# Threshold attention feeding an attention mixture of experts on one core: a new work order, a third pair of score banks at first, additions as reductions, masks in a row

## The chip, the cores and the metric

The kernel runs on one core of one Trainium2 chip. The metric is the device time of one execution in microseconds. A core has a matrix engine (TensorE, PE in the profile; its weight loads are PEld), a vector engine (VectorE, DVE), an activation engine (ScalarE, ACT), a general engine (GpSimd, POOL) and a queue engine (SyncE, SP) that issues DMAs. Matrix products are written to PSUM, which has eight banks of 128 partitions x 512 f32 values.

## The reference

Eight batches, eight heads, 576 rows, 64 values a head. The first stage is attention in which a score counts only when it lies within `tau` of its row's maximum. Its output, 576 x 512 a batch, is the input of the second stage: four experts, each a causal attention with its own projections, of which every row uses two.

```python
def _attn_ref(q, k, v, tau):
    scores = scale * np.matmul(q, k.transpose(0, 1, 3, 2))
    thresh = np.max(scores, axis=-1, keepdims=True) - tau
    scores = np.where(scores >= thresh, scores, -1000000000.0)
    ...
    attn = np.exp(scores)
    attn = attn / (np.sum(attn, axis=-1, keepdims=True) + 1e-09)
    return np.matmul(attn, v)

def _moe_ref(x, w_gate, wq, wk, wv, wo):
    logits = x @ w_gate
    topk = np.argpartition(-logits, K, axis=-1)[..., :K]
    ...
    for e in range(E):
        q = x @ wq[e]
        ...
        scores = scale * (q @ k.transpose(0, 2, 1))
        scores = np.where(causal, -1000000000.0, scores)
        ...
        ye = a @ v @ wo[e]
        ...
            out += mask[..., None] * w[:, :, kk:kk + 1] * ye
```

## The kernel before

**Tiling.** Two heads make a head pair; there are 32 (`n` = 0 to 31, four a batch). The 576 rows are four tiles of 128 and a tail of 64; the tails of both heads share one tile (tile 4). The order of the tiles is `TS` = 4, 2, 3, 0, 1, and `TS0` for the first pair.

**First stage**, for each pair: `load` (DMAs of q, k, v), `prep` (transposes of k and q, split into a high and a low f32r part by `hi` on ScalarE and `lo` on VectorE, and spread by DMAs to `kt` and `qt`), then `scores` for each tile. `scores` has, for each head: matmuls into a score buffer of two banks (`s_main`, or `s_tail` for the tail); the row maximum (`s_max`, L889, VectorE; scores carry a minus sign, so it is a minimum); exp on ScalarE (`s_exp`, L901); the threshold (`s_thr`, L894: an addition of `tau_p`, one for both heads); the masked multiply, which also adds up the rows (`s_stt`, L906, VectorE); the sum plus 1e-9 (`add_eps`, L911), its reciprocal (`inv`, L915); the division on GpSimd (`s_nrm`, L919); transposes on TensorE (L774) and their evacuation to `pt` and `ptt` (L763 on ScalarE, L765 on VectorE). `attnv` multiplies groups of tiles, (4, 2, 3) and (0, 1), with v. These matmuls have 64 output columns and stand side by side in the array: form 128\*64 in the profile, `cols="C"` in the code. All others are of form 128\*128, `"F"`, except the very first scores, `"R"`.

**Second stage**, `second(b)`, once a batch: projections (`proj`, `values`), the gate, scores of two experts at a time (`s2`: for each expert two f32r matmuls and, accumulated onto them, one bf16 matmul that adds the causal mask), maximum (`max2`, L1107), exp with row sums (`exp2`, L1115), `add_eps` and `inv` again, the scaling on GpSimd (`scale2`, L1135), transposes, `av2` (form 128\*64), and the output projection.

**Order.** The order of all instructions is written out by a planner. `work` makes a list of tasks, each with an engine, a time, dependencies, buffers and a due time `pri`, counted in fifths of a head pair: five units a pair, 20 a batch. `plan` runs them through a clock of its own: an engine that becomes free takes the ready task with the smallest `pri` for which buffers are free. On TensorE a task of another form than the last has `STICK` added to its `pri`, and when it is taken, `SWITCH` (ns) is added to its start. `PR` holds one offset for each kind of task, `PR0` corrections for the first four pairs; `PJ`, `VJ`, `S2J` and `TAILK` space the tasks of the second stage. The emitted order is fixed; on the chip, semaphores alone decide when an instruction starts.

**PSUM.** `Space.pick` gives banks: a score buffer (class `s`) takes a pair of neighbouring banks out of the first `SCAP` = 4, any other buffer (class `g`) one of the banks from `GFROM` = 4. `LEAVE` banks must stay free when scores take theirs. `EARLY` = 0.0, so the two other limits in these lines are not used.

**Other buffers.** `SLOTS` has the counts: 10 `pt`, 5 `ptt`, 4 `pp`, 8 `sm`. An `sm` is a 128 x 8 tile of row statistics: maxima in columns 0 and 1, sums in 2 and 3, thresholds in 4 and 5. The weights of the second stage are loaded in four parts, from `W_FROM` on, `W_EACH` apart, in the planner's ns.

Of the kernel before, what the change touches and what calls it, by code (L numbers as in the profile page):

```python
# [20 lines left out]
EPS = 1e-9  # L21

B, H, S, D = 8, 8, 576, 64
E = 4
# [56 lines left out]
CROSS, LATE, SELF, DRAIN, SWITCH, BEGIN = 40.0, 171.0, 36.0, 168.0, 120.0, 800.0  # L81


class Space:
# [177 lines left out]
def work(K):  # L262

    tasks = []

    def task(eng, t, fn, deps=(), pri=0.0, takes=(), uses=(), cols=None, ld=0.0, name="", at=0.0):
        t = t if isinstance(t, dict) else {eng: t}
        x = Task({e: (u[0] - u[1], u[0]) for e, u in t.items()}, fn, deps, pri, takes, uses, cols, ld, name, at)
        tasks.append(x)
        return x  # L270
# [34 lines left out]
    def load(n):  # L305
# [5 lines left out]
        dk = [dma(lambda j=j: K.load_k(n, j), (), pri, [ki], name=f"ldk{n}") for j in range(2)]  # L311
        dk.append(dma(lambda: K.load_kt(n), (), pri, [kit], move=144.0, name=f"ldk{n}"))
        dq = [dma(lambda j=j: K.load_q(n, j, e), (), pri + 0.01, [qi], name=f"ldq{n}", e=e) for j in range(2)]
        dq.append(dma(lambda: K.load_qt(n, e), (), pri + 0.01, [qit], move=144.0, name=f"ldq{n}", e=e))
        at = 20000.0 * n
        dv = [dma(lambda: K.load_v(n, vm), (), pri + 2, [vm], move=736.0, at=at, name=f"ldv{n}")]
        for j in range(2):
            dv.append(dma(lambda j=j: K.load_vt(n, vm, j), (), pri + 2, [vm], move=72.0, at=at, name=f"ldv{n}"))
# [3 lines left out]
        sc = task("DVE" if n == 0 else "POOL", (270, 30), lambda: K.scale_qt("DVE" if n == 0 else "POOL"), dq[2:], 5 * (n - 1) - 1, [], [qit], name=f"qs{n}")  # L322
# [10 lines left out]
    def prep(n):  # L333
# [4 lines left out]
        m = pe(4 * TR, lambda: K.tr_main(g, "k"), dk[:2], p0, [g, hl], [ki], ld=30.0, name=f"qkT{n}")  # L338
        hk, lk = split(g, slice(KO + ST, KO + ST + SM), [m], p0, hl, SM, f"hl{n}")
        g2 = Buf("g")  # L340
        m2 = pe(2 * TR, lambda: K.tr_tail(g2), [dk[2], sc], p0 + 0.5, [g2], [kit, qit], ld=30.0, name=f"qkTt{n}")
# [888 lines left out]
```

## Time and profile before

| what | value |
|---|---|
| median of three runs | 964.48 us |
| lowest, highest | 963.38, 966.53 us |
| profiled execution | 962.86 us |
| its span | 961.1 us |
| PE busy in it | 925.4 us, 9372 matmuls |
| DVE busy | 786.1 us, 2211 instructions |
| ACT busy | 629.6 us |
| POOL busy | 365.8 us |

The span runs from the first to the last instruction of the profiled execution. Busy times are sums over the whole span; a matmul's end is modelled, and the matmuls overlap, so a busy PE need not be at its peak. In rows of the timeline the columns are start, length, engine, line, operation, output<-input, shapes and count; neighbouring instructions of one kind are merged into one row, and what stands in brackets is the idle time before it and what ended it. In rows of the groups they are line, engine, operation, names and shapes, count, then busy time in us and mean length in ns, then the idle time before them and what ended it. A row of the waits has the waiting engine, tile and line, what it waited for, and total us, times and longest us. L774 and L777 are the helpers that issue every transpose and every other matmul, L763 and L765 every copy.

### The profile page before, as it was taken

Reading aid. Unit: us, or ns where it says so; the run is one execution under the profiler, and the core shown is the slowest. Engines: PE = TensorE matmul, PEld = TensorE weight load, DVE = VectorE, ACT = ScalarE, POOL = GpSimd, SP = SyncE. Lnnn points to the kernel's source line nnn. Section 1 sums busy time; section 2 is a strip of 40 time slices with the busy share of each in tenths; the row PEclk is TensorE's granted clock in tenths of the full one; section 3 lists DMA queues with packets and bytes.
Section 4 is the critical chain, followed back from the end, with each engine's and each line's share of the span. In section 5 each row is a group of like instructions: output and inputs, shape, how many; then the busy total and the mean of one; then the engine's idle time right before and its main releaser. Section 6 shows DMA issues by size and latency. Waiting matters only on the chain.

```text
span 961.1 us, 26069 instructions
## 1 busy us (share of the span) xinstructions
PE 925.4 (96%) x9372; PEld 847.2 (88%) x9372; DVE 786.1 (82%) x2211; ACT 629.6 (66%) x1468; POOL 365.8 (38%) x637
## 2 busy tenths in 40 slices
PE   5878999999999999999999999999999999999997
PEld 4767899989998899988999899998999889998985
DVE  4889888898888888888798987989888888888453
ACT  3677657676676666666676766766667676676454
POOL 2456334334243433434244433434324343343222
PEclk9999999999999999999999999999999999999999
DMA  6667663545646464554537466354564545531241
GB/s 143 150 174 167 155 152 88 133 102 156 148 118 145 106 151 117 136 144 113 138 90 170 109 153 150 87 128 118 152 153 109 134 105 149 129 95 45 60 113 61
DMA packets 148335, 121.26 MB, mean 126 GB/s; under 512 B 98288, under 2 KB 106480, under 8 KB 148208
## 3 DMA queue, kind: packets, MB, share of 16 engines
q1 hardware_dynamic: 146864, 119.31, 50.9%
q8 instruction: 75, 1.23, 0.6%
q10 hardware_dynamic: 1344, 0.30, 0.2%
q14 instruction: 52, 0.43, 0.1%
HBM read 30.42 MB, written 9.44 MB: 41 GB/s over the span
## 4 chain that ended last, share of the span: by engine, by line
PE 75%; DVE 17%; ACT 2%; issue 2%; DMA 1%; POOL 1%; SPq 0%; ACTq 0%; DVEq 0%; POOLq 0%
PE g L777 42%; PE g L774 19%; PE s L777 14%; DVE sm L889 5%; DVE pp L906 4%; DVE sm L1107 2%; DVE pt L765 1%; DVE sm L911 1%; ACT pt L763 1%; POOL pp L919 1%; DVE ptt L765 0%; DVE gs L1063 0%; DMA qit<-in_q_dram 0%; DMA ob<-in_moe_wv_dram 0%; DVE x L771 0%
## 5 line engine op out<-in xcount | busy, mean ns | idle before, releaser
L919 POOL TENSOR_SCALAR pp<-pp,sm 128x576 f32<-128x576 f32 x288 | 212.7, 749 | 320.4 <-DVE sm L915 238.1
L889 DVE TENSOR_REDUCE sm<-s 128x1 f32<-128x576 f32 x304 | 228.0, 753 | 31.7 <-PE s L777 20.2
L906 DVE SCALAR_TENSOR_TENSOR pp<-s,sm,pp 128x576 f32<-128x576 f32 x288 | 228.2, 815 | 18.2 <-ACT pp L901 8.6
L901 ACT ACTIVATE pp<-s,sm 128x576 f32<-128x576 f32 x288 | 213.8, 743 | 38.1 <-DVE sm L889 32.4
L763 ACT ACTIVATE pt<-g 128x512 f32<-128x512 f32 (+2 forms) x315 | 176.7, 583 | 77.3 <-PE g L774 74.2
L774 PE MATMUL g<-ident,pp 128*128 128x128 f32 x1312 | 192.7, 276 | 11.8 <-POOL pp L919 4.3
L777 PE MATMUL s<-kt,qt 128*128 128x288 f32 x1016 | 195.7, 315 | 6.9 <-DVE pp L906 6.6
L774 PEld LDWEIGHTS g<-ident,pp 128*128 128x128 f32 x1312 | 153.2, 141 | 22.1 <-POOL pp L919 7.8
L777 PEld LDWEIGHTS s<-kt,qt 128*128 128x128 f32 x1016 | 147.1, 191 | 15.3 <-issue 4.3
L777 PE MATMUL g<-pt,vm 128*64 128x128 f32 (+1 forms) x2560 | 156.0, 264 | 0.0
L777 PEld LDWEIGHTS g<-pt,vm 128*64 128x64 f32 x2560 | 132.9, 137 | 6.0 <-issue 4.5
L1135 POOL TENSOR_SCALAR p<-p,sm,gw 128x256 f32<-128x256 f32 (+4 forms) x144 | 89.8, 633 | 109.0 <-DVE sm L894 44.8
L777 PE MATMUL g<-x,wh 128*128 128x288 f32 x512 | 107.1, 302 | 0.0
L1115 ACT ACTIVATE p<-g,sm 128x512 f32<-128x512 f32 (+3 forms) x128 | 66.7, 527 | 33.2 <-DVE sm L1107 13.2
L777 PEld LDWEIGHTS g<-x,wh 128*128 128x128 f32 x512 | 81.5, 189 | 0.1
L777 PE MATMUL g<-x,wl 128*128 128x288 f32 x256 | 75.5, 295 | 0.0
L763 ACT ACTIVATE x<-g 128x320 fp32r<-128x320 f32 x64 | 26.2, 410 | 71.3 <-PE g L777 71.2
L771 DVE TENSOR_TENSOR x<-g,x 128x320 fp32r<-128x320 f32 x64 | 29.2, 456 | 48.4 <-ACT x L763 48.4
L765 DVE COPY pt<-g 128x512 f32<-128x512 f32 (+1 forms) x85 | 55.8, 658 | 15.3 <-PE g L774 14.0
L777 PE MATMUL g<-wh,x 128*128 128x260 f32 x320 | 65.0, 290 | 0.1
L777 PE MATMUL g<-qq 128*128 128x512 f32 (+3 forms) x256 | 61.8, 352 | 1.5 <-ACT p L1115 0.5
L774 PE MATMUL g<-ident,p 128*128 128x128 f32 x400 | 62.0, 279 | 0.9 <-POOL p L1135 0.9
(125 smaller groups left out, 1474.1 us busy)
## 6 DMA issues: line engine op xcount, KB each, us to landing
kt<-hl SPq DMA_DIRECT2D x248, 144.0 KB, 2.6
qq<-k SPq DMA_DIRECT2D x64, 256.0 KB, 4.4
qt<-hl SPq DMA_DIRECT2D x124, 128.0 KB, 2.5
ki<-in_k_dram SPq DMA_DIRECT2D x64, 128.0 KB, 3.3
vm<-in_v_dram SPq DMA_DIRECT2D x32, 256.0 KB, 3.1
qq<-q SPq DMA_DIRECT2D x64, 128.0 KB, 2.3
out_dram<-ob SPq DMA_DIRECT2D x32, 256.0 KB, 2.2
qi<-in_q_dram SPq DMA_DIRECT2D x62, 128.0 KB, 2.7
```

The costliest lines, as they stand in the source:

```text
L763: self.nc.scalar.activation(dst, src, AF.Copy)
L765: self.nc.vector.tensor_copy(dst, src)
L771: eng.tensor_tensor(dst, a, b.bitcast(F32), op=ALU.subtract)
L774: self.nc.tensor.transpose(out, x, self.ident)
L777: self.nc.tensor.matmul(out, x, y, start=first, stop=last)
L889: self.nc.vector.tensor_reduce(self.small(sm)[:, j:j + 1], self.dbank(s)[:, :, :HS], axis=AX.XY, op=op, negate=neg)
L901: self.nc.scalar.activation(e, self.dbank(s)[:, :, :HS], AF.Exp, bias=self.small(sm)[:, j:j + 1], scale=-1.0)
L906: self.nc.vector.scalar_tensor_tensor(e, self.dbank(s)[:, :, :HS], m[:, 4 + j:5 + j], e, op0=ALU.is_le, op1=ALU.mult, accum_out=m[:, 2 + j ...
L919: self.nc.gpsimd.tensor_scalar(p, p, self.small(sm)[:, 2 + j:3 + j], 0.0, op0=ALU.mult, op1=ALU.add)
L1107: self.nc.vector.tensor_reduce(o, v, axis=AX.X, op=ALU.max, negate=True)
L1115: self.nc.scalar.activation(self.p2(p2)[:, j * SM:j * SM + w], self.bank(gs[j])[:, o:o + w], AF.Exp, bias=m[:, j:j + 1], accum_out=m[:, 2 ...
L1135: self.nc.gpsimd.tensor_scalar(p, p, self.small(sm)[:, 2 + j:3 + j], g[:, o:o + 1], op0=ALU.mult, op1=ALU.mult)
```

## The change

Six things are changed.

1. **Prices and penalties of the planner**: `SWITCH`, `STICK`, `TAILK`, `PJ`, `S2J`, `TS0`, `W_FROM`, `W_EACH`, `LEAVE`.
2. **Due times**: `TUNE` holds some 400 corrections, one for a kind of task and a phase (the pair's place in the batch, in the first batch apart; first, middle or last batch), or a kind and a part (tile, expert pair). `tuned` looks them up by the task's name, which therefore gets separators, and `task` adds them to `pri`.
3. **Banks**: up to 56.7 us of the planner's clock, scores have three pairs (banks 0 to 5) and other buffers the banks 6 and 7; afterwards two pairs and four banks, as before. Banks 4 and 5 come from a pool of their own, which is closed and opened anew with single banks at the first use by a `g` buffer.
4. **Additions**: an `sm` is now a standing tile of 128 x 16, in which `tau` and 1e-9 are written once, next to each maximum and each sum. `s_thr` and `add_eps` become a `tensor_reduce` with `add` over two neighbouring values (`pairs`).
5. **Set-up**: GpSimd writes 1e-9 into the eight `sm` tiles (a memset each) and `tau` (two one-column operations each); the two VectorE operations for `tau_p` go.
6. **Masks**: `s2` issues the score matmuls of both experts first and then both mask matmuls. Where both experts share a bank (`nar`), the start flag is on the first expert's first matmul alone.

```diff
-CROSS, LATE, SELF, DRAIN, SWITCH, BEGIN = 40.0, 171.0, 36.0, 168.0, 120.0, 800.0
+CROSS, LATE, SELF, DRAIN, SWITCH, BEGIN = 40.0, 171.0, 36.0, 168.0, 172.0, 800.0
...
-            pairs = [i for i in range(0, SCAP if now > EARLY else 6, 2) if ok[i] and ok[i + 1]]
+            pairs = [i for i in range(0, 4 if now > EARLY else 6, 2) if ok[i] and ok[i + 1]]
...
-        one = [i for i in range(GFROM if now > EARLY else 2, 8) if ok[i]]
+        one = [i for i in range(4 if now > EARLY else 6, 8) if ok[i]]
...
+    def tuned(name):
+
+        if "/" in name:
+            f, b, *part = name.split("/")
+            phase = "a" if b == "0" else "z" if int(b) == B - 1 else "m"
+        elif "." in name:
+            f, n, *part = name.split(".")
+            phase = ("a" if int(n) < NPAIR else "") + str(int(n) % NPAIR)
+        else:
+            return 0.0
+        return TUNE.get(f"{f}|{phase}", 0.0) + (TUNE.get(f"{f}.{part[0]}", 0.0) if part else 0.0)
...
+        pri += tuned(name)
...
-                a = pe(2 * (f32r(2, w) + 68), lambda: K.s2(gs, nar, qq, t, w), sp, pri, list(dict.fromkeys(gs)), [qq], name=f"s2{b}")
+                a = pe(f32r(4, w) + 165, lambda: K.s2(gs, nar, qq, t, w), sp, pri, list(dict.fromkeys(gs)), [qq], name=f"s2/{b}/{ep}{t}")
...
-PJ = 0.62
+PJ = 0.619
 VJ = 0.56
-S2J = 1.29
-TAILK = 0.36
-STICK = 0.59
+S2J = 1.289
+TAILK = 0.733
+STICK = 0.794
...
+TUNE = {'sk2|a': -2.42, 'sk2|m': -1.16, 'sk2|z': 11.93, 'qs|a3': 10.37, 'max.4': 2.28, 'exp|2': 3.69,
...
-W_FROM = 31527.09
-W_EACH = 10736.66
+W_FROM = 35537.903
+W_EACH = 14490.379
 T2S = (3, 4, 2, 1, 0)
-TS0 = (2, 4, 3, 0, 1)
-LEAVE = 1
-SCAP = 4
-GFROM = 4
-EARLY = 0.0
+TS0 = (2, 4, 3, 1, 0)
+LEAVE = 0
+EARLY = 56700.0
...
+        self.third = tc.tile_pool(name="ps3", bufs=1, space=PSUM)
+        self.pool3, self.begun = self.third.__enter__(), EARLY > 0.0
...
-        self.tau_p = const([P, 2], F32, "tau_p")
-        for j in range(2):
-            nc.vector.tensor_scalar(self.tau_p[:, j:j + 1], tau_t, 0.0, None, op0=ALU.max)
...
+        self.sms = [const([P, 16], F32, f"sm{i}") for i in range(SLOTS["sm"])]
+        for t in self.sms:
+            nc.gpsimd.memset(t[:, 5:8:2], EPS)
...
+        for t in self.sms:
+            for j in range(2):
+                nc.gpsimd.tensor_scalar(t[:, 2 * j + 1:2 * j + 2], tau_t, 0.0, 0.0, op0=ALU.max, op1=ALU.add)
...
+            if buf.cls in "sg" and buf.slot in (4, 5):
+                if buf.cls == "g" and self.begun:
+                    self.third.__exit__(None, None, None)
+                    self.third, self.begun = self.tc.tile_pool(name="ps4", bufs=1, space=PSUM), False
+                    self.pool3 = self.third.__enter__()
+                pool = self.pool3
...
+    def pairs(self, sm, out, o, nj):
+
+        m = self.small(sm)
+        self.nc.vector.tensor_reduce(m[:, out:out + nj], m[:, o:o + 2 * nj].rearrange("p (j k) -> p j k", k=2), axis=AX.X, op=ALU.add)
...
-        self.nc.vector.tensor_tensor(m[:, 4 + a:4 + b], m[:, a:b], self.tau_p[:, a:b], op=ALU.add)
+        self.pairs(sm, 8 + js[0], 2 * js[0], len(js))
...
-    def add_eps(self, sm, o, nj):
-        x = self.small(sm)[:, o:o + nj]
-        self.nc.vector.tensor_tensor(x, x, self.eps[:, :nj], op=ALU.add)
...
+    def add_eps(self, sm, nj):
+        self.pairs(sm, 10, 4, nj)
...
-                self.mm(g[:, o:o + w], u[:, j, t * P:w], u[:, 2 + 2 * j + x, :w], x == 0, False)
-            self.mm(g[:, o + t * P:o + w], self.ident_b, self.mask, False, True)
+                self.mm(g[:, o:o + w], u[:, j, t * P:w], u[:, 2 + 2 * j + x, :w], x == 0 and not (nar and j), False)
+        for j in range(2):
+            o = j * w if nar else 0
+            self.mm(self.bank(gs[j])[:, o + t * P:o + w], self.ident_b, self.mask, False, j == 1 or not nar)
```

More of the change, by code (lines that the diff above doesn't have):

```diff
@@ L321, in load @@
         VMB[n] = vm
-        sc = task("DVE" if n == 0 else "POOL", (270, 30), lambda: K.scale_qt("DVE" if n == 0 else "POOL"), dq[2:], 5 * (n - 1) - 1, [], [qit], name=f"qs{n}")
+        sc = task("DVE" if n == 0 else "POOL", (270, 30), lambda: K.scale_qt("DVE" if n == 0 else "POOL"), dq[2:], 5 * (n - 1) - 1, [], [qit], name=f"qs.{n}")
         LD[n] = (ki, qi, kit, qit, vm, dk, sc, dv, dq)
@@ L355, in prep @@
                 sk[j] = [dma(lambda j=j, r=r: K.spread_k(hl, kt, j, r, None), tl if j == 0 else tl[:4],
-                             p0 + 1.6 + 0.1 * j, [kt], [hl], name=f"sk{n}", move=1288.0) for r in range(2)]
+                             p0 + 1.6 + 0.1 * j, [kt], [hl], name=f"sk.{n}", move=1288.0) for r in range(2)]
             else:
@@ L393, in scores @@
         th = [task("DVE", SMALL, lambda js=js: K.s_thr(sm, js), [ms[j] for j in js], i + PR["thr"], [], [sm],
-                   name=f"thr{n}_{s}") for js in ([[0, 1]] if nj == 2 and ONETHR else [[j] for j in range(nj)])]
+                   name=f"thr.{n}.{s}") for js in ([[0, 1]] if nj == 2 and ONETHR else [[j] for j in range(nj)])]
         for j in range(nj):
             ns.append(task("DVE", (825, 75), lambda j=j: K.s_stt(bufs[j], sm, pp, j), [es[j], th[j if len(th) > 1 else 0]], i + PR["stt"], [],
-                           [bufs[j], sm, pp], name=f"stt{n}_{s}"))
-        a = task("DVE", SMALL, lambda: K.add_eps(sm, 2, nj), ns, i + PR["sum"], [], [sm], name=f"sum{n}_{s}")
-        r = task("DVE", SMALL, lambda: K.inv(sm, 2, nj), [a], i + PR["sum"], [], [sm], name=f"inv{n}_{s}")
-        nr = [task("POOL", (750, 25), lambda j=j: K.s_nrm(sm, pp, j), [r, ns[j]], i + PR["nrm"] + 0.01 * j, [], [sm, pp], name=f"nrm{n}_{s}")
+                           [bufs[j], sm, pp], name=f"stt.{n}.{s}"))
+        a = task("DVE", SMALL, lambda: K.add_eps(sm, nj), ns, i + PR["sum"], [], [sm], name=f"sum.{n}.{s}")
+        r = task("DVE", SMALL, lambda: K.inv(sm, nj), [a], i + PR["sum"], [], [sm], name=f"inv.{n}.{s}")
+        nr = [task("POOL", (750, 25), lambda j=j: K.s_nrm(sm, pp, j), [r, ns[j]], i + PR["nrm"] + 0.01 * j, [], [sm, pp], name=f"nrm.{n}.{s}")
               for j in range(nj)]
@@ L530, in gate @@
             for step, e in K.gate_steps(lg, gs, gw):
-                d = task(e, (218, 110) if e == "ACT" else (180, 84), step, [d] if d else vs, pri, [gs, gw], [lg], name=f"gate{b}")
+                d = task(e, (218, 110) if e == "ACT" else (180, 84), step, [d] if d else vs, pri, [gs, gw], [lg], name=f"gate/{b}")
             return d
```

152 lines of the change are left out of this document (76 added, 76 removed).

## The prediction, made before the changed kernel ran

> **What bounds the kernel now.** I read the stretches first (busy time of each engine between two times), then the chain that ended last, then the order on TensorE, then the waits.
>
> ```profile
> PE 75%; DVE 17%; ACT 2%; issue 2%; DMA 1%; POOL 1%; SPq 0%; ACTq 0%; DVEq 0%; POOLq 0%
> ```
> ```profile
> 0.00:60.00 60.00, 42.73 (x363) 36.69 (x363) 42.00 (x113) 32.05 (x64) 23.58 (x57) 1.00 0.65 153
> 60.00:115.00 55.00, 48.39 (x494) 42.67 (x495) 49.76 (x125) 42.21 (x90) 31.09 (x55) 1.00 0.66 161
> 115.00:229.00 114.00, 112.90 (x1171) 104.55 (x1170) 99.75 (x284) 76.50 (x180) 45.10 (x77) 1.00 0.54 132
> ...
> 686.00:800.00 114.00, 113.19 (x1164) 104.28 (x1164) 97.23 (x276) 77.08 (x179) 42.15 (x72) 1.00 0.53 129
> 800.00:880.00 80.00, 79.85 (x833) 74.89 (x832) 65.89 (x188) 53.02 (x123) 29.58 (x48) 1.00 0.45 110
> 880.00:961.00 81.00, 74.42 (x687) 64.56 (x685) 40.12 (x123) 40.65 (x119) 19.91 (x34) 1.00 0.26 69
> ```
> The columns are the stretch, its length, then PE, PEld, DVE, ACT and POOL busy (with instructions), the granted clock, DMA share and GB/s. There are three regimes. From 115 to 880 us TensorE is bound: it is idle 5.0 us in the six rows of 114 or 115 us (first and last shown) and 0.15 us after them, and VectorE has 14 to 17 us to spare in each. Before 115 us TensorE is idle 17.3 + 6.6 = 23.9 us; only the first stage exists there, and VectorE, at 49.8 of 55 us in the second row, is the tighter engine. After 880 us it is idle 6.6 us. The clock column is 1.00 everywhere, so it plays no part. In the middle only less TensorE work, or a better packed order, saves time; at first, what VectorE holds up.
>
> **The masks.** On TensorE, in the middle of a batch:
>
> ```profile
> 369.38 0.69 PE L777 MATMUL g<-qq 128*128 128x512 f32 x2
> 369.91 0.23 PE L777 MATMUL g<-mask,ident_b 128*128 128x128 bf16 x1
> 369.95 0.71 PE L777 MATMUL g<-qq 128*128 128x512 f32 x2
> 370.50 0.23 PE L777 MATMUL g<-mask,ident_b 128*128 128x128 bf16 x1
> 370.66 1.09 PE L777 MATMUL g<-pt,vm 128*64 128x128 f32 x16
> 371.59 0.39 PE L777 MATMUL g<-ptt,vt 128*64 128x128 f32 x4
> 371.81 1.04 PE L777 MATMUL g<-pt,vm 128*64 128x128 f32 x16
> 372.68 0.39 PE L777 MATMUL g<-ptt,vt 128*64 128x128 f32 x4
> 373.00 1.06 PE L777 MATMUL s<-hl,qd 128*128 128x288 f32 x6
> ...
> 379.57 0.23 PE L777 MATMUL g<-mask,ident_b 128*128 128x128 bf16 x1
> 379.63 0.28 PE L774 MATMUL g<-ident,pp 128*128 128x128 f32 x1
> ```
> ```profile
> L777 PE MATMUL g<-mask,ident_b 128*128 128x128 bf16 x128 | 29.5, 230 | 0.0
> ```
> Only starts are used, since ends are modelled. One head costs 370.50 - 369.91 = 0.59 us from mask to mask. A 512-column matmul costs 0.23 us (951.46 to 951.70 below, the same width), so two are 0.47 and the mask 0.12 us. The 128 masks are 64 pairs of heads. In a row, the first mask of a pair no longer stands before an f32r matmul. No row shows a mask behind a mask. The bounds: the second costs nothing (0.12 saved) or the whole 0.12 (nothing). The nearest row of one-pass 128-column work is 16 matmuls in 370.66 to 371.59, 0.058 us each; I take 0.06. So 64 x 0.06 = **3.8 us** saved, between 0 and 7.7, all where TensorE is bound.
>
> **The mode changes.** The same rows price them. Leaving the 128*64 form: 372.68 to 373.00 is 0.32 us for four matmuls that take 0.22 inside it (371.59 to 371.81), so 0.10. Entering: mask to 128*64 is 0.16 us, mask to transpose 0.06 (379.57 to 379.63), so 0.10. A round trip costs 0.20 us. I counted 93 of them on TensorE's timeline; the first and last:
>
> ```profile
> 33.84 1.09 PE L777 MATMUL g<-pt,vm 128*64 128x128 f32 x16
> ...
> 951.46 0.40 PE L777 MATMUL g<-wol,z 128*128 128x512 f32 x1
> 951.70 0.40 PE L777 MATMUL g<-woh,z 128*128 128x512 f32 x1
> 952.02 1.09 PE L777 MATMUL g<-pt,v 128*64 128x128 f32 x16
> ```
> That is 18.6 us of TensorE. There are 64 first-stage and 80 second-stage groups of this form, 144, so 51 already ride behind another. The penalty on changing form rises from 0.59 to 0.794 units; 20 units are one batch of about 114.6 us, so the planner's patience grows from 3.4 to 4.5 us, a third. The higher SWITCH in the planner's clock itself only shifts its dates. A third more rides are 17: 17 x 0.20 = **3.4 us**. Ends: none, and half the trips (9.3). What hides the delay of a group is slack in its evacuation and its `pt` slots (10, for 9 a head pair); if that is gone, the transposes behind wait.
>
> In a sentence apart, the Trainium skill, TensorEngine Tiling (Array Packing), Key Properties, says that changing the tiling mode drains the array; the trace agrees with 0.20 us a round trip, and gives the price that the page lacks.
>
> **The additions.** thr (L894) and sum (L911) become reductions over two values.
>
> ```profile
> L911 DVE TENSOR_TENSOR sm<-sm,eps 128x2 f32<-128x2 f32 (+1 forms) x240 | 51.2, 213 | 4.8 <-ACT p L1115 2.1 <-ACT p L1128 1.1
> L894 DVE TENSOR_TENSOR sm<-sm,tau_p 128x2 f32<-128x2 f32 (+1 forms) x160 | 28.5, 178 | 2.1
> L1081 DVE TENSOR_REDUCE gs<-gw 128x5 f32<-128x20 f32 x8 | 1.4, 174 | 0.0
> ```
> ```profile
> 54.36 1.47 POOL L919 TENSOR_SCALAR pp<-pp,sm 128x576 f32<-128x576 f32 x2 [1.61 <-PE g L774]
> 55.15 0.68 DVE L894 TENSOR_TENSOR sm<-sm,tau_p 128x1 f32<-128x1 f32 x1
> ...
> 56.80 0.16 DVE L911 TENSOR_TENSOR sm<-sm,eps 128x1 f32<-128x1 f32 x1
> ```
> Such an addition takes 0.16 us by itself and 0.68 when it starts inside a GpSimd pass over `pp`: both rows end at 55.83. So the 400 additions, 79.7 us, hold about 79.7 - 400 x 0.16 = 16 us of this. The nearest reduction, 20 values to 5, takes 0.174 us; at that price 400 cost 70 us if no wait remains, 10 us less VectorE work; if the wait stays, 6 us more. From 115 us on neither reaches the end, because VectorE has over 14 us to spare a batch: cost nothing. If that cover were gone, 10 us in eight batches would be 1.2 us each. Before 115 us they count:
>
> ```profile
> L894 DVE TENSOR_TENSOR sm<-sm,tau_p 128x2 f32<-128x2 f32 (+1 forms) x24 | 6.3, 262 | 0.6
> L911 DVE TENSOR_TENSOR sm<-sm,eps 128x2 f32<-128x2 f32 (+1 forms) x23 | 4.3, 188 | 0.5
> ```
> Those 47 take 10.6 us there against 8.2 at 0.174, so up to 2.4 us; it goes into the sum of the start.
>
> Apart from the sum, two pages of the Trainium skill speak here. VectorE: DVE Perf Modes, Rules for kernel authors, calls `tensor_reduce` on a hot path the slowest of VectorE's operations and says to restructure; by it the start would lose about 0.7 us (47 x 0.014) instead. SBUF — State Buffer, Who interferes with whom, says that an instruction with two SBUF inputs is locked out while GpSimd reads SBUF, and that on trn2 `tensor_reduce` never is; by it the start gains the 2.4. The row that ends with GpSimd's speaks for the second; no row here shows a tiny reduction beside a GpSimd pass.
>
> **The third pair of score banks.** Up to the planner's 56.7 us, scores own three pairs and everything else two banks; before, two pairs and four banks.
>
> ```profile
> PE s L777 <- DVE pp L906: 7.6, 6, 2.6
> ```
> ```profile
> PE s L777 <- DVE pp L906: 1.3, 3, 0.6
> ```
> ```profile
> 11.92 1.12 PE L774 MATMUL g<-ident,ki 128*128 128x128 f32 x4
> ...
> 15.54 1.78 PE L777 MATMUL s<-qq,qd 128*128 128x288 f32 x6 [2.50 <-DVE pp L906]
> 16.63 1.46 POOL L919 TENSOR_SCALAR pp<-pp,sm 128x576 f32<-128x576 f32 x2 [11.60 <-DVE sm L915]
> ```
> These are waits in 0 to 60 and in 60 to 115 us: scores wait for the masked multiply (L906) to free a pair, in the clearest case 2.5 us at 15.54, and VectorE has no next maximum meanwhile. A free third pair removes much of the 7.6; next late is VectorE itself. With up to 2.4 us from the additions and a replanned order of maxima and evacuations, I take **6 us** of the 23.9. Ends: 12 saved (half the idle time; the load of K ahead of the first transpose and VectorE's own work keep the rest), and a loss, the third rival.
>
> **The rest.** Set-up adds 8 memsets and 16 one-column GpSimd operations, and takes two VectorE ones away. By the nearest rows that is under 4 us:
>
> ```profile
> L767 POOL TENSOR_SCALAR wh<-sm 128x4 fp32r<-128x4 f32 x4 | 0.8, 198 | 1.0 <-DMA sm<-in_moe_w_gate_dram 1.0
> ```
> GpSimd's first work then is the 16.63 row, after 11.6 us idle, which hides it: nothing, or 3 us if the first maximum waited for all of it. Weights are loaded up to 15 us later; their last load now lands near 83 us and is first needed at 112.44:
>
> ```profile
> 80.85 2.37 DMA ob<-in_moe_wq_dram
> ```
> ```profile
> 112.44 0.51 PE L777 MATMUL g<-x,wh 128*128 128x288 f32 x2
> ```
> Hidden, with 14 us left. The due times of some 400 task kinds move with no new work: in the middle they can at most close the 5.0 us of idle time and what hides in stretched transposes, or open more. I take **3 us** (2 lost to 7 saved); in the last batch **0.7 us** of 6.6 (3 either way).
>
> **Sum.** 3.8 + 3.4 + 6 + 3 + 0.7 = 16.9. The profiled execution took 962.86 us, of which 961.1 is the span and 1.8 lies around it: 962.9 - 16.9 = 946.0. The median, 964.48, is 1.6 above it: **947.6**.
>
> **Rivals.**
> 1. *Only the masks pay.* The order comes out no better: TensorE was already 113 of 114 us busy, the chain already ran through it, and rides may be limited by slots instead of patience. Then 3.8 and some 1 us of mode changes: 962.9 - 4.8 + 1.6 = 959.7. That the dearer mode changes don't do what they say (93 trips stay) belongs here.
> 2. *The order packs much better*: the start gives 12, mode changes 5, the middle 5, the end 3, masks 3.8: 28.8, 935.7. For it: transposes wait for GpSimd and evacuations in places; against: five gains at once.
> 3. *Two banks at first are too few* (slower). Holding times: a four-transpose block 0.45 us, its evacuation 0.6 (row below), hand-offs 0.2.
>
> ```profile
> L763 ACT ACTIVATE pt<-g 128x512 f32<-128x512 f32 (+2 forms) x315 | 176.7, 583 | 77.3 <-PE g L774 74.2
> ```
> Nine such blocks, five tails (0.6), three of preparation (1.75) and two attn-v groups (3.4) are about 27 us of bank a head pair, of 40 that two banks give in the 20 us of a pair. It decides from about 0.7 us of extra holding for each of the 19. Past that every block waits; at 0.2 us for each of 53 blocks in 56.7 us, 10.6 us: 962.9 + 10.6 - 3.8 + 1.6 = 971.3. Against it: ScalarE is busy 32 of the first 60 us and takes evacuations soon.
>
> **Chances.** Forecast (936 to 957) 0.62; rival 1 (957 to 961.5) 0.17; rival 2 0.06; rival 3 0.08; small gains and losses that cancel 0.07. A measurement of this kernel tells 0.3%, 2.9 us, from no change. Faster by more: 0.62 + 0.17 + 0.06 less a little of rival 1, 0.83; within 0.09; slower 0.08. The range 936 to 962 leaves out rivals 2 and 3 and part of the cancelling.
>
> **What would show it.** Masks: two bf16 matmuls in a row, 0.06 us from start to start, in 64 places. Mode changes: about 76 entries into the 128*64 form. Additions: mean near 0.17 us with none over 0.3. Start: score waits on L906 below 2 us before 60 us, and the first projection near 106 instead of 112.44. Wrong if the entries stay near 93, if score waits are replaced by transposes waiting for ScalarE, or if the six middle stretches show more idle time than 5 us.

## The result, and the profile after

The changed kernel takes **949.21 us** (median of 4 runs, 948.63 to 953.02) against 964.03 us of the kernel before (median of 4 runs, 963.38 to 966.53): a ratio of 0.985, with a 95% interval of 0.9819 to 0.9881. The forecast was 947.6 us in a range of 936 to 962. So the total came out; its terms did not, as the rest shows. The profiled execution took 949.27 us, of which the span is 947.5.

From the page of the changed kernel: the span, the busy times, the chain that ended last.

```profile
span 947.5 us, 26120 instructions
...
PE 912.1 (96%) x9372; PEld 847.1 (89%) x9372; DVE 762.4 (80%) x2176; ACT 631.4 (67%) x1501; POOL 368.2 (39%) x661
...
PE 76%; DVE 11%; DMA 6%; SPq 3%; ACT 2%; issue 2%; POOL 1%; DVEq 0%; POOLq 0%; ACTq 0%
```

The same 9372 matmuls, 13.6 us less span. VectorE's share of the chain fell from 17 to 11%; the additions on that share, as e2 shows, are worth half of the gain. DMA and SP's queue together have grown from 15 to 78 us of the chain: 34 of them before 100 us, the rest in the middle and in the last batch, where the chain now runs through some loads of q and k and some of the DMAs that spread them, and before it ran through none. The table of due times moves these transfers too; what that costs in the middle was not tested.

The stretches of the changed kernel (stretch, length, then PE, PEld, DVE, ACT, POOL busy, granted clock, DMA share, GB/s):

```profile
0.00:60.00 60.00, 41.18 (x314) 34.75 (x314) 39.94 (x113) 34.06 (x67) 26.64 (x81) 0.94 0.66 149
60.00:115.00 55.00, 51.04 (x562) 46.70 (x561) 44.17 (x119) 41.15 (x90) 31.02 (x57) 1.00 0.73 167
115.00:229.00 114.00, 112.98 (x1179) 105.71 (x1178) 99.60 (x288) 80.52 (x190) 46.42 (x78) 1.00 0.57 134
...
686.00:800.00 114.00, 112.48 (x1180) 105.87 (x1179) 96.65 (x274) 78.37 (x187) 43.48 (x75) 1.00 0.54 129
...
880.00:947.50 67.50, 62.64 (x576) 54.97 (x571) 27.32 (x85) 30.96 (x95) 15.48 (x28) 1.00 0.32 81
```

Idle time of TensorE hardly moved: 22.8 us before 115 us (23.9 in the kernel before), 7.3 us in the six middle stretches, of which the first and the last are shown (5.0), 4.9 us at the end (6.6, over a longer stretch). By that view nothing was gained in the middle. But stretches that end at fixed times don't hold the same work in both kernels. Two points of the work do: the first matmul of the first projection, and the first one of the last batch's. The first one, before and after, from TensorE's timeline:

```profile
107.61 0.46 PE L777 MATMUL g<-x,wh 128*128 128x288 f32 x2
```
```profile
104.72 0.53 PE L808 MATMUL g<-x,wh 128*128 128x288 f32 x2
```

The matmul at 112.44 us, which the prediction called the first, was not the first; its milestone is 107.61. Cut at those two points, the spans of the profiled executions are:

| kernel | start, to the first projection | middle, to that of the last batch | tail | span |
|---|---|---|---|---|
| before | 107.6 | 796.2 | 57.3 | 961.1 |
| after | 104.7 | 785.5 | 57.3 | 947.5 |
| e2, additions alone | 108.8 | 789.4 | 57.3 | 955.5 |
| e3, additions and masks, old order | 106.9 | 788.9 | 56.8 | 952.6 |
| e1, masks alone | 108.7 | 798.1 | 56.9 | 963.6 |
| e4, masks apart, new order | 106.4 | 783.0 | 57.5 | 946.8 |
| e5, additions with two inputs, new order | 104.4 | 789.6 | 57.3 | 951.3 |
| e6, K loaded first | 104.1 | 783.6 | 57.4 | 945.1 |

So 2.9 us came from the start, **10.7 us from the middle**, and nothing from the tail. Each row is one execution, and the table itself shows how far a row can be trusted. Up to the first projection e1 does the same work in the same order as the kernel before, e3 the same as e2, and e4 the same as the changed kernel; yet their starts differ by 1.1, 1.9 and 1.7 us. In the middle e6 does the same as the changed kernel, and differs by 1.9 us. The 10.7 us stand; the 2.9 us are uncertain by about 2.

A busy TensorE hides waits, since the ends of matmuls are modelled: the middle became 10.7 us shorter with the same number of matmuls in it, and by the view of the stretches its idle time still rose. In e2, whose matmuls come in the order of before, the middle is 6.8 us shorter, while the page shows only 2.9 us less busy time in all (922.5 against 925.4).

Two more views carry what follows. The additions, as the page of the changed kernel has them:

```profile
L789 DVE TENSOR_REDUCE sm<-sm 128x2 f32<-128x4 f32 (+1 forms) x400 | 56.0, 151 | 12.5 <-ACT p L1145 3.1
```

And the masks of two experts on its TensorE, in the middle of a batch:

```profile
250.52 1.17 PE L808 MATMUL g<-qq 128*128 128x512 f32 x4
251.54 0.28 PE L808 MATMUL g<-mask,ident_b 128*128 128x128 bf16 x2
251.75 1.09 PE L808 MATMUL g<-pt,vm 128*64 128x128 f32 x16
```

The 400 additions take 0.151 us each where they took 0.199 (79.7 us over 400). Four score matmuls and both masks take 251.75 - 250.52 = 1.23 us; before they took 370.66 - 369.38 = 1.28. Counted over TensorE's timeline, entries into the form 128\*64 fell from 93 to 83.

### The profile page after: what moved, and what is told of

Same layout as the page of the kernel before. It is cut to its first block, busy times and chain, and to the rows that moved or that the text cites. A ratio compares the mean times of both kernels' runs of the same rounds, so it can differ in the third digit from the quotient of the medians.

```text
span 947.5 us, 26120 instructions
## 1 busy us (share of the span) xinstructions
PE 912.1 (96%) x9372; PEld 847.1 (89%) x9372; DVE 762.4 (80%) x2176; ACT 631.4 (67%) x1501; POOL 368.2 (39%) x661
## 3 DMA queue, kind: packets, MB, share of 16 engines
q8 instruction: 75, 1.23, 0.6%
## 4 chain that ended last, share of the span: by engine, by line
PE 76%; DVE 11%; DMA 6%; SPq 3%; ACT 2%; issue 2%; POOL 1%; DVEq 0%; POOLq 0%; ACTq 0%
PE g L808 41%; PE g L805 20%; PE s L808 15%; DVE pp L935 4%; DVE sm L920 3%; SPq L811 3%; DMA qq<-k 2%; DMA qit<-in_q_dram 1%; DVE sm L1137 1%; DMA ki<-in_k_dram 1%; ACT pp L930 1%; DMA ob<-in_moe_wk_dram 1%; DVE hl L868 1%; DVE sm L789 1%; DMA kt<-qq 0%
## 5 line engine op out<-in xcount | busy, mean ns | idle before, releaser
L794 ACT ACTIVATE pt<-g 128x512 f32<-128x512 f32 (+2 forms) x299 | 170.6, 583 | 61.6 <-PE g L805 58.5
L805 PE MATMUL g<-ident,pp 128*128 128x128 f32 x1312 | 197.8, 276 | 6.7 <-POOL pp L947 2.3
L1165 POOL TENSOR_SCALAR p<-p,sm,gw 128x512 f32<-128x512 f32 (+4 forms) x144 | 89.3, 628 | 119.3 <-DVE sm L943 48.3
L796 DVE COPY pt<-g 128x512 f32<-128x512 f32 (+1 forms) x101 | 65.1, 654 | 9.5 <-PE g L805 7.8
L789 DVE TENSOR_REDUCE sm<-sm 128x2 f32<-128x4 f32 (+1 forms) x400 | 56.0, 151 | 12.5 <-ACT p L1145 3.1
L1137 DVE TENSOR_REDUCE sm<-g 128x1 f32<-128x512 f32 (+2 forms) x96 | 56.1, 594 | 6.9 <-PE g L808 6.7
```

The lines of the kernel that those rows point to most:

```text
L789: self.nc.vector.tensor_reduce(m[:, out:out + nj], m[:, o:o + 2 * nj].rearrange("p (j k) -> p j k", k=2), axis=AX.X, op=ALU.add)
L794: self.nc.scalar.activation(dst, src, AF.Copy)
L796: self.nc.vector.tensor_copy(dst, src)
L805: self.nc.tensor.transpose(out, x, self.ident)
L1137: self.nc.vector.tensor_reduce(o, v, axis=AX.X, op=ALU.max, negate=True)
L1165: self.nc.gpsimd.tensor_scalar(p, p, self.small(sm)[:, 10 + j:11 + j], g[:, o:o + 1], op0=ALU.mult, op1=ALU.mult)
```

## The experiments

The theory after the result: the masks and the mode changes shorten TensorE's own work as forecast, but the additions pay too, since VectorE's spare time is an average. The rival is the prediction's own account: additions pay at the start alone, masks in full. All times are medians. The kernel before was timed again beside each set of experiments (964.64 us with e1, e2, e3 and e11; 963.75 with e4 to e7; 963.36 with e8 to e10; 963.76 with e12), and the ratio is to that.

### e1: the masks alone, on the kernel before

```diff
-                self.mm(g[:, o:o + w], u[:, j, t * P:w], u[:, 2 + 2 * j + x, :w], x == 0, False)
-            self.mm(g[:, o + t * P:o + w], self.ident_b, self.mask, False, True)
+                self.mm(g[:, o:o + w], u[:, j, t * P:w], u[:, 2 + 2 * j + x, :w], x == 0 and not (nar and j), False)
+        for j in range(2):
+            o = j * w if nar else 0
+            self.mm(self.bank(gs[j])[:, o + t * P:o + w], self.ident_b, self.mask, False, j == 1 or not nar)
```

> The kernel before in its own order, with both masks of two heads in a row. Theory: 64 pairs x 0.06 us of TensorE, 964.0 - 3.8 = 960.2 us, and the stretches of 114 us in the middle hold a little more work each. Rival (the next wait takes it back, since the order was planned around the masks apart): within 1 us of 964.0.

964.52 us, ratio 0.9997 (0.9986 to 1.0008): nothing, where 3.8 us had been forecast. Yet TensorE's own work did fall. On e1's timeline:

```profile
370.56 1.16 PE L777 MATMUL g<-qq 128*128 128x512 f32 x4
371.55 0.28 PE L777 MATMUL g<-mask,ident_b 128*128 128x128 bf16 x2
371.77 1.09 PE L777 MATMUL g<-pt,vm 128*64 128x128 f32 x16
```

The group takes 1.21 us instead of 1.28. Over all 64 groups, from the first score matmul to the matmul behind the masks, it is 52.6 us instead of 55.9: 3.3 us less, near the 3.8 of the forecast. The middle got no shorter by it (798.1 us against 796.2). At this place the chain of e1 (start, length, what) says why the 0.07 us bought nothing:

```profile
369.32 0.76 DVE sm L889
370.08 0.65 DVE gs L1063
...
376.33 0.67 DVE sm L889
...
377.43 2.03 PE g L774 x17
```

From 369.32 to 377.43 us the chain runs through VectorE, but for 0.45 us of ScalarE and about as much of issue; the masks at 371.55 lie beside it. TensorE was nearly always busy there, and still not what set the time.

### e2: the additions alone, in the old order

The edit is the `pairs` reduction with its standing `sm` tiles and the set-up, and every constant of the planner as in the kernel before; the masks stay apart.

```diff
-        self.nc.vector.tensor_tensor(m[:, 4 + a:4 + b], m[:, a:b], self.tau_p[:, a:b], op=ALU.add)
+        self.pairs(sm, 8 + js[0], 2 * js[0], len(js))
...
```

> The order of before, masks apart, one addition as a reduction in place of each addition of two inputs (with the set-up that goes with it). Theory (only the start is short of VectorE): mean of the 400 near 0.16 us with none over 0.3, VectorE 15 us less busy, and 0 to 2.4 us less time, 962.8. Rival 1 (a reduction is the slowest operation, 0.174 us or more and still held up by GpSimd): 964.7. Rival 2 (VectorE's late answers hold up TensorE in the middle too): 5 us or more less, 959 or below.

957.01 us, ratio 0.9914 (0.9898 to 0.993): **7.6 us from an edit that the forecast had given nothing outside the start.** The second rival of the expectation came true: the middle gained 6.8 us. At the start no gain shows (108.8 us against 107.6), but one execution can't decide that: in e2's, the granted clock was 0.50 from 28.3 to 31.7 us and 0.51 from 62.4 to 65.9, and in that of the kernel before it didn't fall. Where the middle lost time, the chain of the kernel before shows, in a stretch that the prediction had looked past:

```profile
306.20 0.69 DVE pt L765
306.89 0.67 DVE sm L889
...
313.04 0.73 DVE pp L906 x2
313.78 0.52 DVE sm L911
...
317.02 0.67 DVE sm L911
...
318.21 0.87 PE g L774 x6
```

Twelve microseconds of the chain, 306.20 to 318.21, are VectorE back to back, and two of its pieces are the tiny addition L911 at 0.52 and 0.67 us. The addition's row on VectorE's timeline, and what GpSimd did then:

```profile
313.69 0.60 DVE L911 TENSOR_TENSOR sm<-sm,eps 128x2 f32<-128x2 f32 x1
```
```profile
313.55 1.48 POOL L919 TENSOR_SCALAR pp<-pp,sm 128x576 f32<-128x576 f32 x2
```

The addition ends at 314.29, where the first of the two GpSimd passes ends (313.55 + 0.74). With the reduction, in e2, the same operation in the same order, also just after a pass has begun on GpSimd:

```profile
313.21 0.15 DVE L789 TENSOR_REDUCE sm<-sm 128x2 f32<-128x4 f32 x1
```
```profile
313.06 1.46 POOL L947 TENSOR_SCALAR pp<-pp,sm 128x576 f32<-128x576 f32 x2
```

0.15 us and no wait. And e2's chain in that stretch is TensorE's, from beginning to end but for two ScalarE copies:

```profile
308.19 1.09 ACT pt L794 x2
...
310.85 3.80 PE g L808 x48
...
316.04 2.01 PE g L805 x18
```

Over the whole chain, from e2's page, VectorE's share fell from 17 to 8%:

```profile
PE 82%; DVE 8%; ACT 4%; issue 2%; POOL 2%; DMA 2%; SPq 0%; ACTq 0%; DVEq 0%; POOLq 0%
```

e2 also has the standing tiles and the set-up; the kind of instruction by itself is tested in e5, in the new order only.

### e3: additions and masks, in the old order

e2 with the masks in a row. The order of instructions is that of the kernel before.

> Masks in a row and additions as reductions together, in the order of before: all of the change except the new order and the third pair of banks. Theory: the two add up, 964.0 - 3.8 - 1.2 = 959.0, so some 10 us of the change are the order's. Rival (the order is nearly worthless and the two edits carry the gain): below 953.

954.62 us, ratio 0.9894 (0.9876 to 0.9911): 10.0 us for both, between the two expectations. The masks, worth 0.1 us alone, seem to bring 2.4 us on top of the additions (957.01 to 954.62), but the intervals overlap. The profiles do not place a gain where the masks are: of the 2.9 us between the spans of e2 and e3, 1.9 lie before the first projection, where both do the same work and e2's clock was low, and 0.5 in the middle. That a saving on TensorE counts once the chain is TensorE's is thus not shown. What the new order and the third pair add is the step from e3 to the changed kernel: 5.4 us in the medians, 4.2 in the ratios (whose intervals touch), 5.1 in the spans, of which 2.2 lie in the start and 3.4 in the middle, with 0.5 lost in the tail.

### e4: the masks apart again, in the new order

```diff
-                self.mm(g[:, o:o + w], u[:, j, t * P:w], u[:, 2 + 2 * j + x, :w], x == 0 and not (nar and j), False)
-        for j in range(2):
-            o = j * w if nar else 0
-            self.mm(self.bank(gs[j])[:, o + t * P:o + w], self.ident_b, self.mask, False, j == 1 or not nar)
+                self.mm(g[:, o:o + w], u[:, j, t * P:w], u[:, 2 + 2 * j + x, :w], x == 0, False)
+            self.mm(g[:, o + t * P:o + w], self.ident_b, self.mask, False, True)
```

> The changed kernel in its own order with the mask of each head right behind its scores again. Theory: 64 x 0.06 us more, 949.2 + 3.8 = 953.0. Rival (the order has slack that hides it): 949 to 950.

950.03 us, ratio 0.9858 (0.9841 to 0.9875): 0.8 us above the changed kernel, less than the intervals tell apart, and the middle of its profile is not longer but 2.5 us shorter (783.0 against 785.5). So the masks gain nothing clear of the noise in any of the three comparisons (0.1, 2.4 and 0.8 us). Only e1's intervals are narrow enough to exclude 3.8 us, and only for the order of before.

### e5: additions with two inputs, in the new order

```diff
-        self.nc.vector.tensor_reduce(m[:, out:out + nj], m[:, o:o + 2 * nj].rearrange("p (j k) -> p j k", k=2), axis=AX.X, op=ALU.add)
+        self.nc.vector.tensor_tensor(m[:, out:out + nj], m[:, o:o + 2 * nj:2], m[:, o + 1:o + 2 * nj:2], op=ALU.add)
```

> The changed kernel in its own order, the additions again with two inputs (two strided columns of the same tile) in place of reductions. Theory (GpSimd's passes hold up some of them, TensorE is bound): the additions are 12 to 20 us longer in sum, with single ones up to 0.75 us, and the time grows by 0 to 2.5 us, about 950.5. Rival 1 (the shape of the operation does not matter, only that the operands lie in one tile): mean 0.16 us, 949.2. Rival 2 (the new order is planned tight around 0.16 us and breaks): 954 or more.

952.62 us, ratio 0.9883 (0.9869 to 0.9898): 3.4 us above the changed kernel, more than the 0 to 2.5 of the theory. The intervals touch (the changed kernel's ends at 0.9881), so the size is uncertain; the middle of its profile is 4.1 us longer. Same values, same order; only the kind of instruction differs. The group on e5's page:

```profile
L789 DVE TENSOR_TENSOR sm<-sm 128x2 f32<-128x2 f32 (+1 forms) x400 | 72.0, 190 | 12.1 <-ACT p L1145 3.4
```

16 us more VectorE work in all cost 3.4 us of time. 38 of the 400 take over 0.3 us, the longest 0.782; of the 400 reductions none takes over 0.159. So the held-up additions hurt in the new order as well, but less than in the old (3.4 against 7.6). Fewer of them lie on the chain: 18 of the 39 over 0.3 us in the kernel before, 11 of the 38 in e5.

### e11 and e7: the third pair of score banks

e11 is e3 with one constant changed; e7 is the changed kernel without its third pair, replanned.

```diff
-EARLY = 0.0
+EARLY = 56700.0
```

> As the run e3_old_order, planned with the old prices and due times, but with three pairs of score banks and two other banks up to 56.7 us of the planner's clock. The order is planned anew, so only the time up to 115 us and the start of the first projection are compared with e3_old_order. Theory (a free third pair helps the start): scores wait less than 2 us for the masked multiply before 60 us, first projection 3 us or more earlier. Rival (two banks for all else are too few): transposes wait for a bank, first projection not earlier or later.

956.1 us, ratio 0.991 (0.9894 to 0.9926), against 954.62 without the pair: no gain, and a first projection at 109.2 instead of 106.9 us, though e3's clock fell to 0.50 for 6.8 us on the way and e11's didn't. The waits of e11 in its first 60 us (waiting engine, tile and line, releaser; total us, times, longest):

```profile
PE s L808 <- DVE pp L935: 3.1, 2, 2.9
PE g L805 <- ACT pt L794: 3.0, 3, 1.3
PE s L808 <- DMA qt<-hl: 2.2, 2, 1.4
```

The waits of scores for a bank fell from 8.2 us (e3) to 3.1, and what replaced them are transposes that wait for ScalarE to free one of the two other banks, and scores that wait for a DMA. That is the prediction's third rival in small.

> The changed kernel planned anew with two pairs of score banks and four other banks from the beginning, all prices and due times of the change kept. Theory (the third pair is worth little at the start): time up to the first projection within 2 us of 104.7, the total moved mostly by what the new planning does later. Rival (it carries the start): scores wait 5 us or more for the masked multiply before 60 us and the first projection comes 4 us or more later.

958.82 us, ratio 0.9947 (0.9931 to 0.9963): 9.6 us above the changed kernel, with its first projection at 111.8 us. The score waits in the first 60 us of e7 and of the changed kernel:

```profile
PE s L808 <- DVE pp L935: 9.0, 5, 2.9
```
```profile
PE s L808 <- DVE pp L935: 2.8, 2, 1.9
```

The same wait as in the kernel before is back. The start of 111.8 us is not the pair's alone: e7's clock was about 0.50 from 30.3 to 33.7, from 50.7 to 61.0 and from 74.6 to 78.1 us, 17.1 us in all, against 6.8 in the changed kernel. And due times made for three pairs now drive an order with two, so 9.6 us is not what the pair is worth; neither is the nothing of e11. What each is worth without the other stays open.

### e8: the due times taken out

```diff
-TUNE = {'sk2|a': -2.42, 'sk2|m': -1.16, 'sk2|z': 11.93, 'qs|a3': 10.37, 'max.4': 2.28, 'exp|2': 3.69,
...
+TUNE = {}
```

> The changed kernel planned anew with an empty table of due times; prices, banks, masks and additions as changed. Theory (the table carries the order): 15 us or more above 949.2, with more entries into the 128*64 form than 83 and the start and the batches both longer. Rival (the prices and the third pair carry it): within 4 us of 949.2.

976.24 us, ratio 1.0131 (1.0117 to 1.0146), with 97 entries into the form 128\*64: 27.0 us above the changed kernel, 21.6 above e3, which has the same additions and masks in the old order. The other constants of the new order, SWITCH, STICK, TAILK and the third pair among them, are worse than the old ones without the corrections that go with them. The order can only be judged as a whole. The table holds 508 corrections, more than the 400 named above. One thing that the new order does with them is easy to count: between e3 and the changed kernel 33 evacuations of PSUM move from VectorE (2209 to 2176 instructions) to ScalarE (1468 to 1501). What these are worth wasn't tested.

### e9 and e10: what a mode change costs

32 extra transposes of the identity into unused columns, one after a product of `attnv`: inside the group of tiles 0 and 1 (e9), where it breaks the form 128\*64 and is left and entered again, or behind the group (e10).

```diff
                 K.av(g, (s - first) * P, vm, PTS[n, s][0], PTS[n, s][1], s)
+                if s == 0:
+                    K.transpose(K.bank(g)[:, 2 * P:3 * P], K.ident)
```

e10 has `s == 1`.

> The changed kernel in its own order, with one extra 128-column transpose (of the identity, into unused columns of the bank) in the middle of each of the 32 attn-v groups of tiles 0 and 1, so that each of these groups is left and entered once more: 32 more entries into the 128*64 form, 32 more matmuls. Theory A (TensorE's time is the kernel's time wherever it is spent): 32 x (0.11 + 0.20) = 9.9 us more, 959.1. Theory B (as the masks showed, part of what TensorE does lies beside a chain through VectorE): less than that, 952 to 957. TensorE's own rows should show 0.20 us a round trip either way.

> As e9_change_inside, with the extra transpose at the end of the group of tiles 0 and 1, where the form changes anyway in most places: 32 more matmuls and few more entries. Theory A: 32 x 0.11 = 3.5 us more, 952.7, so that e9 and e10 differ by 6.4 us. Theory B: 949.5 to 952, and a difference of 2 to 5 us.

e10: 952.66 us, ratio 0.9889 (0.9876 to 0.9902), 91 entries. e9: 955.95 us, ratio 0.9916 (0.99 to 0.9931), 115 entries. The price in TensorE's time stands on e9's timeline:

```profile
369.35 0.39 PE L810 MATMUL g<-ptt,vt 128*64 128x128 f32 x4
369.67 0.33 PE L807 MATMUL g<-ident 128*128 128x128 f32 x1
369.93 1.09 PE L810 MATMUL g<-pt,vm 128*64 128x128 f32 x16
```

The four matmuls before the transpose take 0.32 us, of which 0.22 are their own: 0.10 to leave the form. The transpose takes 0.26, of which 0.11 is its own (a block of four takes 0.45): 0.15 to enter. So 0.25 us a round trip, a little above the 0.20 that the prediction worked out. The 24 trips more of e9 over e10 are then 6.0 us of TensorE; the time rose by 3.3 us, uncertain by about 2. About half of it came through, by these bounds between a quarter and nine tenths. e10 meets Theory A's number, but with 8 trips (2 us) more than that sum has.

### e6: K loaded first

The new due times put the loads of v ahead of those of k in SP's queue. From the changed kernel, SP's timeline and TensorE's first matmul:

```profile
0.80 0.45 SPq L811 DMA_DIRECT2D vm<-in_v_dram  x1
2.28 1.22 SPq L811 DMA_DIRECT2D vt<-in_v_dram  x2
3.54 1.28 SPq L811 DMA_DIRECT2D ki<-in_k_dram  x2
```
```profile
7.18 1.09 PE L805 MATMUL g<-ident,ki 128*128 128x128 f32 x4 [7.18 <-DMA ki<-in_k_dram]
```

K is issued 2.74 us later than if it were first, and TensorE starts at 7.18 us instead of 5.67. The edit moves one task to the head of the order:

```diff
-        for t in plan(work(em)):
+        order = plan(work(em))
+        first = [t for t in order if t.name == "ldk.0"]
+        for t in first + [t for t in order if t not in first]:
```

> The changed kernel with one move: the three loads of k for the first pair are issued ahead of the loads of v, as before the change; the rest of the order is the same. Theory (the first transpose waits for k): first matmul at 5.7 instead of 7.2 us, and TensorE may stay above the activity that keeps its clock, which was 0.5 for 6.8 us at 20 us: 1.5 to 3 us less, 946.9. Rival (the next thing late is the set-up on GpSimd, which ends at 8 us, or q): no change, 949.2.

**947.29 us**, ratio 0.9829 (0.9816 to 0.9842): the fastest of all in the median, 1.9 us below the changed kernel, though the intervals overlap. From e6's stretches, and its first matmul on TensorE's timeline:

```profile
0.00:60.00 60.00, 43.00 (x326) 35.55 (x328) 42.10 (x118) 36.07 (x71) 29.03 (x85) 1.00 0.68 154
```
```profile
5.75 1.08 PE L805 MATMUL g<-ident,ki 128*128 128x128 f32 x4 [5.75 <-POOL sm L749]
```

That matmul starts 1.43 us earlier, and the first 60 us hold 12 matmuls more than in the changed kernel. But the first projection comes only 0.6 us earlier (104.1 against 104.7 us), and the other 1.9 us between the spans lie in the middle, where nothing was changed. So a gain in time from K first is likely but not shown.

### e12: the conversions of the weights later, on top of e6

The prediction had called the loads of the weights hidden. The chain of the changed kernel runs through three of them:

```profile
39.40 2.60 DMA ob<-in_moe_wk_dram
...
61.73 4.00 DMA ob<-in_moe_wk_dram
...
88.23 2.74 DMA ob<-in_moe_wq_dram
```

The projections don't need them so early. But ScalarE and GpSimd convert each weight after its load, in the fixed order of their queues, and stand still if the load isn't there: 8.3 us in all before 115 us (6.3 in the kernel before), with evacuations and divisions queued behind. The edit sorts the emitted order anew, with these conversions 2 us later:

```diff
+def later(order, ns):
...
+        k = t.start if t.name != "ldk.0" else 0.0
+        if t.name == "w" and t.by in ("ACT", "POOL"):
+            k += ns
...
-            t.fn()
+        for t in later(order, 2000.0):
+            t.fn()
```

> K first as in e6_k_first, and the conversions of the loaded weights (ScalarE's high part, GpSimd's scaling and low part) placed 2.0 us of the planner's clock later in their engines' queues, behind 1 to 6 tasks of the first stage each; their own order and their buffers' stay. Theory now: weights are not hidden as the prediction had it. In e6 and in the changed kernel ScalarE and GpSimd stand 8 to 10 us in all before these conversions, waiting for the load, with evacuations and divisions queued behind, and the chain runs through three of the loads. Then those waits fall to 3 us or less, the first projection comes 1.5 to 4 us earlier (100 to 102.6 us instead of 104.1), and the time falls to 943.5 to 946 us. Rival, the prediction's own step: the loads are hidden, since their last one is needed only at 104 us; then 947.3 us as e6, within 1 us, though the waits go. A second rival: conversions that come later hold the two staging buffers longer and delay the next loads past the first projection: 948.5 to 951 us, with the first projection after 105 us.

948.53 us, ratio 0.9838 (0.9822 to 0.9855), first projection at 104.96 us: no gain over e6, as the prediction's own step has it. The second rival's range begins at 948.5 us, with a first projection after 105 us; the run lies on the edge of both, so the two are not told apart. The waits fell only from 9.6 to 7.2 us and not to 3, so the test is weaker than meant. The last load took the place of the others in e12's chain:

```profile
94.39 4.66 DMA ob<-in_moe_wv_dram
```

No gain from 2 us of delay was seen; whether the loads cost time at the start at all stays open.

## Why the prediction was right in its total and wrong in its parts

| step | forecast, us | what the runs showed, us |
|---|---|---|
| masks | 3.8 | 3.3 of TensorE (e1); of time 0.1 alone, 2.4 on top of the additions, 0.8 in the new order, none clear of the noise |
| mode changes | 3.4 (17 trips) | 10 trips; 2.5 of TensorE, about 1.4 of time |
| additions outside the start | 0 | 6.8 in the middle (e2) |
| start | 6 | 2.9, uncertain by about 2; no gain by the additions seen |
| due times, middle and last batch | 3.7 | not separable; new order and third pair together 5.4 |

**Additions: the step failed that says "From 115 us on neither reaches the end, because VectorE has over 14 us to spare a batch: cost nothing".** The 14 us are a sum over a stretch of 114 us. Within it VectorE works 8 to 12 us on end (306.20 to 318.21 in the chain of the kernel before) and carries the chain while it does. An addition of 0.16 us that waits 0.5 us for GpSimd lengthens such a stretch by 0.5 us, whatever time is free later. e2 shows that the edit pays in the middle, and e5 that the kind of instruction does in the new order. The prediction had the right row in hand (0.68 us inside a GpSimd pass, 16 us of such waits in all) and then dropped it in the middle for an average. The bound from its own numbers would have been the 79.7 - 70 = 10 us less VectorE work; 7.6 us came.

The choice between the two pages of the Trainium skill came out as the prediction had it. SBUF — State Buffer, Who interferes with whom, says that an operation with two SBUF inputs is shut out while GpSimd reads and `tensor_reduce` never is; the trace agrees, with 38 of 400 over 0.3 us in e5 and none in the changed kernel. VectorE: DVE Perf Modes, Rules for kernel authors, has `tensor_reduce` as the slowest; at these sizes the measurement differs, 0.151 us against 0.16 for an addition that nothing holds up.

**Masks: the size was right, and the step failed that puts them "all where TensorE is bound".** The prediction took TensorE's idle time of 5.0 us in 685 for proof that TensorE sets the pace everywhere in the middle. Some 3.3 us of work went (55.9 to 52.6 over the 64 groups), and the time stayed (e1): where the chain was followed, it ran through VectorE beside the masks. Why the masks bring little even with the additions, where the chain is 82% TensorE's (e2), stays open.

**Mode changes: the direction was right, the count too high.** 83 entries instead of about 76. The price of 0.20 us was near (0.25), but the time it buys is about half of it (e9 against e10); the prediction counted it whole. The estimate of 1.4 us is 10 x 0.25 x 3.3 / 6.0, carried over from added trips to removed ones, and no run took away trips alone.

**Start: right in kind, half in size.** The score waits fell from 7.6 to 2.8 us instead of below 2, and the first projection came at 104.7. But the milestone was misread: measured from the 107.61 that was really the first, the gain is 2.9 of the forecast 6, uncertain by about 2. A sign named for being wrong showed in part: transposes that wait for ScalarE, none in the first 60 us before, are 2.6 us there now. Three things were missed. The moved due times put v ahead of k on SP, which delayed the first matmul by 1.5 us; the prediction said that moved tasks bring no new work and didn't look where they went in SP's queue. The additions showed no gain at the start (e2; a small one would be hidden by its clock). And TensorE ran at half speed there, though the clock column says 1.00: of the prediction's own rows, six score matmuls of 288 columns take 1.78 us at 15.54 and 1.06 at 373.00.

**Due times: the sign that was to show them wrong did show.** More than 5 us of idle time in the middle stretches was named as such a sign; there are 7.3, and the middle is 10.7 us shorter all the same. It was a poor sign, since a busy TensorE hides waits, as the result's part shows. That they matter is shown (e8, 27 us), and e11 and e7 fit with their carrying the third pair; how 5.4 us divide between better packing, fewer entries and the third pair stays open. Set-up was hidden, but barely: in e6 the first matmul waits, by the profile, for a GpSimd operation of the set-up until 5.75 us, the time at which K had freed it before (5.67). That the weights are hidden because the last of them is needed late was too short an argument, since their conversions stand in two queues (e12); a price for it wasn't found.

That the total was right is luck: errors of both signs met. Of the 14.8 us that came, the additions alone bring 7.6, which the forecast had left out; the other 7.2 stand where it had 16.9, in the masks, the mode changes, the start and the due times. Of the rivals, the one in which only the masks pay had it the wrong way round; the one with too few banks shows in e11, where its waits come up without deciding the whole.

## What to carry to other kernels

An engine's spare time over a long stretch says nothing about an instruction on it: follow the chain of waits through one whole period, and price an edit where the chain runs through that engine, tiny instructions too. Where TensorE is busy all the time but another engine stands in the chain, a saving on TensorE can come to nothing; price it by the chain, not by the busy time. Read a milestone of the start from more than one execution: the same work differed by up to 1.9 us here. For small sums and additions of row statistics beside a GpSimd that reads SBUF, an instruction with one input is the better choice, and after a replanned order the DMA queues are worth a look, first at their head.

## What the runs showed of the hardware

**TensorE is slow at first, and the clock column doesn't say so.** Four score matmuls of 288 columns take 0.77 us in one place and 1.30 us in another. From the changed kernel, its TensorE timeline and the stretch around it:

```profile
18.43 0.77 PE L808 MATMUL s<-kt,qt 128*128 128x288 f32 x4 [1.93 <-DVE pp L935]
20.96 1.30 PE L808 MATMUL s<-kt,qt 128*128 128x288 f32 x4 [1.75 <-DMA kt<-qq]
```
```profile
19.70:26.50 6.80, 5.09 (x22) 4.71 (x23) 4.37 (x15) 3.29 (x6) 2.52 (x4) 0.50 0.54 132
```

There the granted clock falls to 0.50 for 6.8 us, after waits of 1.9 and 1.75 us. In e6 the column reads 1.00 throughout, and yet:

```profile
17.15 1.30 PE L808 MATMUL s<-kt,qt 128*128 128x288 f32 x4 [1.93 <-DVE pp L935]
...
24.95 0.77 PE L808 MATMUL s<-kt,qt 128*128 128x288 f32 x4
```

So e6 ran at half speed from its first matmul until about 24 us, and the column shows only a fall after a rise. The prediction's sentence that the clock plays no part holds from there on, not at the start. The Trainium skill, TensorE: Matmul & The Clock Gate, What's actually happening, says that the throttled state is the default and that steady work lifts it; the trace agrees, with 1.30 against 0.77 us, and shows that a first rise came 9 to 18 us after the first matmul here, with waits of 1 to 2 us between matmuls. Which executions rise early and fall again differs between kernels of the same order: the kernel before rises at 23.7 us and shows no fall, e3 rises at 18.7 and falls from 25.5 to 32.3. In all, TensorE ran at half speed for 18.0 us before the first projection in the kernel before, 15.9 in the changed kernel, 22.7 in e2, 19.9 in e3 and 29.8 in e7. So a part of the differences between the starts compared above is that.

**Two masks in a row cost 0.07 us from start to start**, a mask ahead of an f32r matmul some 0.12 by the prediction's rows: the second of a pair is nearly half price.

**A two-input addition of two values a row can take 0.78 us**, about the length of a GpSimd pass over 576 values (0.751 us in the mean), and 0.15 when it is left alone (e5).
